# Two edits to a fused recurrence-and-MLP kernel: GpSimd's queue for output packing and half of the stores, 16-bit top bits for the weights

## The chip, the cores and the metric

The kernel runs on one core of a Trainium2 chip. Its engines are called by their profile names: PE (TensorE matmul; PEld is its weight load), DVE (VectorE), ACT (ScalarE), POOL (GpSimd) and SP (SyncE, which here only issues DMAs). Each engine works through its own list of instructions in order and waits on semaphores for the others. A DMA is issued from the list of one engine; here SP and ACT issue all of them. The metric is device time in microseconds (us) of one execution; lower is better.

## The reference

Two blocks in a row. The first is a gated linear recurrence over 4 batches, 8 heads, 768 steps, head size 48; the second a SwiGLU MLP over the 3072 resulting tokens (model width 384, hidden width 1536):

```python
f = 1.0 / (1.0 + np.exp(-f_logit))
for t in range(S):
    state = f[:, :, t, :, None] * state + np.einsum('bhd,bhe->bhde', k[:, :, t], v[:, :, t])
    y[:, :, t] = np.einsum('bhd,bhde->bhe', q[:, :, t], state)
x = y.transpose(0, 2, 1, 3).reshape(B * S, H * D)
g = x @ w_gate
out = (g * (1.0 / (1.0 + np.exp(-g))) * (x @ w_val)) @ w_out
```

q, k, v, f_logit and the output are 32-bit floats. The three weight matrices arrive as 64-bit floats and are turned into 32-bit floats on the core.

## The kernel before

**Chunks and units.** Time is cut into 6 chunks (c = 0 to 5) of 128 steps. For each chunk and each batch b (0 to 3) one "unit" of attention is computed, and then the MLP of the chunk's 512 tokens. Within a unit the recurrence is written as products: scan the gates backward (L576) and forward (L598), scale k and q by the results (L584, L604), multiply them into scores (L617), mask these on DVE (L631), and add the part of the state carried from the chunk before. A unit's function `attention` is a generator; each `yield` is a point where other work is put between.

**Chunk 0 and 1, and the weights.** The attention of chunk 0 runs alone at the start. Then the plain MLP of chunk 0 (`mlp_plain`, L755 and L769, then L778) runs with the attention of chunk 1 and the conversion of the weights around it. A piece of weights is fetched as pairs of 32-bit words into one of 4 buffers (L449, issued by SP), ACT makes two tiles of it, `up` (the low word's contribution, L461) and `top` (the absolute value of the high word, L463), and DVE joins them: clamp (L469), shift and mask (L471), set the sign and the top exponent bit from the high word (L473), and add `up` (L475). In this stretch a scheduler orders the instructions of each engine by its own estimates, so an edit can move neighbours.

**Chunk 2 on (c >= SQUARES).** Now the order of every engine, POOL and SP included, is the order in which the program text puts it (`in_order`), and that follows a planner's list of due times (`CHAINS`, `SCORES`, `times`). PE runs the MLP of the chunk before, as 15 products per hidden triple (`mlp_fifteen`, L957) and then seven products for the way down (`down_seven`: `one`, `six`, `two`, `three`, `four`, `five`, `seven`; L1056 and L1119), with the attention of the present chunk put between.

**How a unit's output reaches the MLP.** For b = 0, 1, 2 the products L652 and L656 leave y in PSUM; ACT copies it into the tile `yT` (L660), and ten DMAs (two of the eight heads straddle a border of 128 rows and go in two pieces) move its pieces of 48, 32 or 16 rows into `xT[c]` (L667), issued by SP. For b = 3 the products go through a block-diagonal tile, `diagonal`: POOL clears it (L544), ACT copies the decayed state into it (two instructions, L546), and PE multiplies (L677). `yT` and `diagonal` share one buffer (tag "x", one copy), so the next writer waits until the ten DMAs of the one before have read it.

**What ACT does behind the diagonal.** ACT's list holds, right after the two copies L546 of chunks 3, 4 and 5, the copy L1082 that empties the single PSUM bank "B" of the products `one` and `two`. The product `four` (seen in the profile as L1056 with the tile `hs`) writes the same bank and starts after that copy.

**POOL and SP.** POOL has little to do from chunk 2 on: a 4-column memset per unit (L605, the gates' first column, which the next unit's backward scan L576 reads) and the diagonal's clear. SP issues, in this order of the text, loads of the squares f, k and q (L428, four DMAs each), of v (L432), a transposition through DRAM for some units (L594, L627), the xT packing (L667), and the stores of half 0 of each block's result (L1065, two DMAs, called from `seven`; half 1 goes out on ACT's queue, called from `five`). An SP DMA that waits holds up all behind it.

Of the kernel before, what the change touches and what calls it, by code (L numbers as in the profile page):

```python
# [9 lines left out]
FP32 = mybir.dt.float32  # L10
I32 = mybir.dt.int32
U32 = mybir.dt.uint32
AF = mybir.ActivationFunctionType
ALU = mybir.AluOpType

# [4 lines left out]
def general_path(ctx, tc, q, k, v, f_logit, moe_w_gate, moe_w_val, moe_w_out, out):  # L20
# [70 lines left out]
    def weight_pieces(dst, src):  # L91
# [9 lines left out]
        def piece(i, j):  # L101
# [13 lines left out]
            nc.vector.tensor_scalar(man, top, 2.0 ** -20, 1.0, op0=ALU.mult, op1=ALU.add)  # L115
            nc.vector.scalar_tensor_tensor(man, lo.bitcast(U32), 2.0 ** -52, man, op0=ALU.mult, op1=ALU.add)
            nc.gpsimd.tensor_tensor(dst[:, i:i + n_a, j:j + n_n], man, p2.bitcast(FP32), ALU.mult)
# [14 lines left out]
    def attention(u):  # L132
        b, c = units[u]
        fr, qr, kr = (raw[nm][u % NRAW] for nm in "fqk")
        nc.scalar.activation(fr[:, :, 0:D], fr[:, :, 0:D], AF.Sigmoid)

# [108 lines left out]
    def mlp(g):  # L245
        h = {}

        def hidden(j):
# [5 lines left out]
            sg = ffn.tile([128, TB], FP32, tag="silu", name="silu", bufs=3)  # L254
            nc.scalar.activation(sg, gp, AF.Silu)
            h[j] = ffn.tile([128, TB], FP32, tag="h", name="h", bufs=16)
# [33 lines left out]
def short_path(ctx, tc, ident, least, judge, q, k, v, f_logit, moe_w_gate, moe_w_val, moe_w_out, out):  # L290
# [9 lines left out]
    nc = tc.nc  # L300
    B, H, S, D = q.shape
    C = 128
    NCH = S // C
# [11 lines left out]
    SQUARES = 2  # L315
# [92 lines left out]
    def squares(nm):  # L408
        return rooms[nm][:, Q:Q + HP * RUN].rearrange("t (a i e) -> t a i e", a=HP, i=NI)[:, :, :, 0:Q]
# [24 lines left out]
    def weight_piece(dst, src, parts):  # L434

        b, a, n = dst.shape[1:]  # L440
        if src.dtype == FP32:
            by_row = src.rearrange("p a (b n) -> p a b n", n=n)
            return (lambda: [nc.sync.dma_start(out=dst[:, :, i], in_=by_row[:, i]) for i in range(a)]), [], []
        shape = [128, b // parts, a, n]
        kept = {}

        def fetch():
            kept["w"] = wst.tile([128, a, 2 * b * n], I32, tag="w64", name="w64", bufs=4)
            nc.sync.dma_start(out=kept["w"], in_=src)  # L449

        def part(m):
            return slice(m * b // parts, (m + 1) * b // parts)

        def halves(m):
            words = kept["w"].rearrange("p a (b n two) -> p a b n two", two=2, n=n)[:, :, part(m)].rearrange("p a b n two -> p b a n two")
            return words[:, :, :, :, 0], words[:, :, :, :, 1]

        def sizes(m):
            lo, hi = halves(m)
            up = wst.tile(shape, I32, tag="up", name="up", bufs=NPART)  # L460
            nc.scalar.activation(up, lo.bitcast(U32), AF.Copy, scale=2.0 ** -29)  # L461
            top = wst.tile(shape, I32, tag="top", name="top", bufs=NPART)
            nc.scalar.activation(top.bitcast(FP32), hi.bitcast(FP32), AF.Abs)  # L463
            kept["up", m], kept["top", m] = up, top

        def join(m):
            lo, hi = halves(m)
            up, top = kept["up", m], kept["top", m]
            nc.vector.tensor_scalar(top.bitcast(FP32), top.bitcast(FP32), as_float(0x38000000), as_float(0x47F00000),  # L469
                                    op0=ALU.max, op1=ALU.min)  # L470
            nc.vector.tensor_scalar(top, top, 3, 0x3FFFFFFF, op0=ALU.logical_shift_left, op1=ALU.bitwise_and)  # L471
            for i in range(b // parts):
                nc.vector.scalar_tensor_tensor(top[:, i], hi[:, i], -(1 << 30), top[:, i], op0=ALU.bitwise_and,  # L473
                                               op1=ALU.bitwise_or)
            nc.vector.tensor_tensor(dst[:, part(m)].bitcast(I32), top, up, ALU.add)  # L475

        return fetch, [lambda m=m: sizes(m) for m in range(parts)], [lambda m=m: join(m) for m in range(parts)]

    def as_float(bits):
        return struct.unpack("<f", struct.pack("<I", bits))[0]  # L480
# [29 lines left out]
    xT = {}  # L510

    def rows_of(par):
        return slice(W * par, W * par + D)
# [3 lines left out]
    def bank(name):  # L517
        return banks[-1].tile([128, 512], FP32, tag="a", name=name)
# [3 lines left out]
    def sigmoid_ahead(u):  # L522


        fr = raw["f"][u % NRAW]
        nc.scalar.activation(fr, fr, AF.Sigmoid)
        ahead.add(u)

    def attention(u):
        b, c = units[u]  # L530
# [17 lines left out]
        def transposed(name, src):  # L548
            p = bank(name)
            for a in range(HP):  # L550
                nc.tensor.transpose(p[:, a * C:(a + 1) * C],
                                    src[:, 2 * a:2 * a + 2, :].rearrange("t r d -> t (r d)"), ident)
            return p.rearrange("p (a t) -> p a t", t=C)

        if c >= SQUARES:
            nc.scalar.activation(squares("f"), squares("f"), AF.Sigmoid)
            if b == (c > SQUARES):

                nc.scalar.activation(spare, spare, AF.Silu)
        else:  # L560
            p = transposed("fTp", fr)
# [9 lines left out]
        if c >= SQUARES:  # L571
# [3 lines left out]
        n = HP * N1  # L575
        nc.vector.tensor_tensor_scan(tail[:, 0:n][:, ::-1], gate[:, 0:n][:, ::-1], floor[:, ::-1], 1.0,  # L576
                                     op0=ALU.mult, op1=ALU.max)
# [9 lines left out]
        if turned:  # L587
# [5 lines left out]
            for r in range(NI):  # L593
                nc.sync.dma_start(out=turn[:, :, :, r, :].rearrange("t i a e -> t (i a) e"),  # L594
                                  in_=beside[Q * r:Q * (r + 1)].rearrange("t i (a e) -> t (i a) e", e=Q))
# [18 lines left out]
        for a in range(HP):  # L614
            for par in range(2):
                r = rows_of(par)
                nc.tensor.matmul(sc[par][:, a * C:(a + 1) * C], lhsT=kT[r, a, :], rhs=qT[r, a, :], start=True, stop=True)  # L617
        if c < NCH - 1 and not turned:
            p = bank("kt")
# [20 lines left out]
        if c and b < B - 1:  # L640

            y = [bank("y") for _ in range(2)]

            def place(a, par):
                return y[par][W * (a % 2):W * (a % 2) + W, a // 2 * C:(a // 2 + 1) * C]

            for a in range(HP):
                for par in range(2):  # L650
                    r = rows_of(par)
                    nc.tensor.matmul(place(a, par), lhsT=decayed[r, a, :], rhs=qT[r, a, :],  # L652
                                     start=a < 2, stop=False, skip_group_check=True)
            for par in range(2):
                for a in range(HP):
                    nc.tensor.matmul(place(a, par), lhsT=v_[:, 2 * a + par, :], rhs=A[:, par, a, :],  # L656
                                     start=False, stop=a >= HP - 2, skip_group_check=True)
            yT = att.tile([128, 2, HP // 2 * C], FP32, tag="x", name="yT")
            for par in range(2):
                nc.scalar.copy(yT[:, par, :], y[par][:, 0:HP // 2 * C])  # L660
            for h in range(H):
                a, par = h // 2, h % 2
                f = h * D
                while f < (h + 1) * D:
                    n = min((h + 1) * D, (f // 128 + 1) * 128) - f
                    r = W * (a % 2) + f - h * D
                    nc.sync.dma_start(out=xT[c][f % 128:f % 128 + n, f // 128, b * C:(b + 1) * C],  # L667
                                      in_=yT[r:r + n, par, a // 2 * C:(a // 2 + 1) * C])
                    f += n
        else:  # L670


            y = bank("y")
            met = set()

            def add(n, lhsT, rhs, last):
                nc.tensor.matmul(y[Q * (n % 4):Q * (n % 4) + Q, n // 4 * C:(n // 4 + 1) * C], lhsT=lhsT, rhs=rhs,  # L677
                                 start=n % 4 not in met, stop=last, skip_group_check=True)
                met.add(n % 4)

            per = 2 * D // Q
            if c:
                for n in range(DM // Q):
                    add(n, diagonal[:, n // per, n % per * Q:(n % per + 1) * Q], qT[:, n // per, :], False)
            flat = v_.rearrange("t h e -> t (h e)")
            for par in range(2):
                for n in range(DM // Q):
                    h = n // per * 2 + par
                    at = n * Q - h * D
                    if -Q < at < D:  # L690
                        add(n, flat[:, W * h + at:W * h + at + Q], A[:, par, h // 2, :], par == 1 or at + Q <= D)
            nc.scalar.copy(xT[c][:, :, b * C:(b + 1) * C], y[:, 0:DM].rearrange("p (a t) -> p a t", t=C))
        yield
        if c < NCH - 1:
            p = bank("dS")
# [212 lines left out]
    def lag(f, *args):  # L908
        lagging.append(lambda: f(*args))  # L909
# [123 lines left out]
    def down_seven(c, h):  # L1033
# [7 lines left out]
        kept = {}  # L1041
# [74 lines left out]
        def seven(n):  # L1116
            p = bank2("o3", "Ao"[n])[:, n, :]
            for j in order:
                nc.tensor.matmul(p, lhsT=hidden_tile(h, j)[:, 2, n * C:(n + 1) * C], rhs=b22[:, j, :], start=j == order[0],  # L1119
                                 stop=j == order[-1])  # L1120
            lag(plus, kept["o", 0][:, n, DH:DM], kept["u5"][:, n, :], p)
            lag(put_out, 0, n, nc.sync)

        return hidden_sums, [(DOWN / 2, lambda f=f, part=part: f(part))
                             for f in (one, six, two, three, four, five, seven) for part in range(2)]
# [237 lines left out]
```

## Time and profile before

| what | value |
|---|---|
| time of the runs without a profile | 609.16, 609.83, 609.94, 610.35; median 609.89 us |
| the profiled execution | 611.35 us, of which the span from first to last instruction is 609.6 us |
| granted TensorE clock | 0.997 |
| ten xT DMAs per unit, 15 units (b = 0, 1, 2 of chunks 1 to 5) | 150 issues, 588 ns median on SP, 1.8 us median to landing |
| stores on SP (L1065) | 10 issues of 192 KB, 2.6 us to landing |
| weight conversion on DVE, L469 + L471 + L473 + L475 | 10.2 + 10.3 + 18.4 + 17.4 us |

The span is what the profile's views describe; the time of a plain run is close to it (0.3 us above). Busy shares are shares of the span. In the groups' view a line reads: line, engine, operation, output<-inputs, shape, count, then busy us and mean ns of one, then idle time of the engine just before, with what ended it. In the timeline a line reads: start, length, engine, line, operation, tiles, shapes, count, and in brackets the idle time just before with what ended it.

### The profile page before, as it was taken

What the parts mean: (1) busy time and instruction counts of PE and PEld (TensorE: products, weight loads), DVE (VectorE), ACT (ScalarE), POOL (GpSimd) and SP (SyncE); (2) the same over time, 40 slices, a digit from 0 to 9 for tenths busy, and PEclk for the clock granted to TensorE, in tenths of its full rate; (3) what the DMA queues carried; (4) which work ended last, traced back from release to release, by engine and by line L of the source; (5) the groups of instructions that cost most, each with busy time, mean ns of one, the idle gap of its engine ahead of it and who ended that gap; (6) DMA issues with size and microseconds to landing.
All of it is one profiled execution on the core that took longest, in us unless ns stands there. A gap on an engine that the chain in (4) does not pass through costs nothing.

```text
span 609.6 us, 10796 instructions
## 1 busy us (share of the span) xinstructions
PE 593.7 (97%) x4036; PEld 488.6 (80%) x4036; DVE 494.5 (81%) x833; ACT 288.6 (47%) x554; POOL 7.5 (1%) x52
## 2 busy tenths in 40 slices
PE   7899999999999999999999999999999999999995
PEld 5744554667888799888899988899988899988895
DVE  7999989868999985999996799996878981666731
ACT  3567544313776512476732376732276731365600
POOL 1000000000000000000000000000000000000000
PEclk9999999999999999999999999999999999999998
DMA  9998372005312045324236344145313100100001
GB/s 203 242 226 282 123 248 78 6 19 159 91 41 73 18 109 125 94 53 96 61 90 148 88 104 106 44 105 127 105 46 84 27 7 9 53 1 1 1 0 59
DMA packets 109142, 54.10 MB, mean 89 GB/s; under 512 B 68760, under 2 KB 102168, under 8 KB 109080
## 3 DMA queue, kind: packets, MB, share of 16 engines
q1 hardware_dynamic: 107064, 50.56, 31.5%
q10 hardware_dynamic: 2016, 2.75, 1.2%
q8 instruction: 34, 0.56, 0.4%
q14 instruction: 28, 0.23, 0.1%
HBM read 44.04 MB, written 6.29 MB: 83 GB/s over the span
## 4 chain that ended last, share of the span: by engine, by line
PE 83%; DVE 10%; SPq 2%; issue 1%; ACT 1%; DMA 1%; POOL 0%; DVEq 0%; ACTq 0%; POOLq 0%
PE o L1056 16%; PE A L957 15%; PE B L957 13%; PE o L957 5%; PE gate L755 5%; PE val L755 5%; PE c L957 5%; PE sc L617 4%; PE o L1119 3%; PE o L778 3%; PE y L677 2%; PE y L656 2%; SPq L667 1%; PE dS L697 1%; PE y L652 1%
## 5 line engine op out<-in xcount | busy, mean ns | idle before, releaser
L1056 PE MATMUL o<-w_out,h 128*128 128x192 f32 x360 | 62.0, 327 | 0.5 <-DVE h L909 0.5
L957 PE MATMUL A<-xs,w_both 128*128 128x256 f32 x240 | 62.1, 381 | 0.0
L1056 PEld LDWEIGHTS o<-w_out,h 128*128 128x128 f32 x360 | 58.7, 190 | 1.7 <-DVE h L909 0.8
L962 ACT COPY c<-A 128x512 f32<-128x512 f32 x40 | 23.3, 583 | 62.7 <-PE A L957 62.7
L962 ACT COPY aside<-A 128x512 f32<-128x512 f32 x60 | 35.1, 585 | 32.5 <-PE A L957 32.5
L858 DVE TENSOR_TENSOR c<-c,aside 128x512 f32<-128x512 f32 x60 | 41.8, 696 | 10.5 <-ACT aside L962 9.0
L957 PEld LDWEIGHTS A<-xs,w_both 128*128 128x128 f32 x240 | 44.9, 190 | 6.5
L909 DVE TENSOR_TENSOR h<-h,c 128x256 f32<-128x256 f32 x100 | 41.4, 422 | 7.3 <-ACT h L973 7.3
L861 DVE TENSOR_TENSOR c<-c,aside 128x512 f32<-128x512 f32 x60 | 41.6, 694 | 2.5 <-ACT aside L962 2.5
L973 ACT ACTIVATE h<-c 128x256 f32<-128x256 f32 x100 | 39.2, 416 | 8.4 <-DVE c L858 5.8
L1056 PE MATMUL o<-ws,h 128*128 128x192 f32 x240 | 41.5, 328 | 0.2 <-DVE A L631 0.2
L957 PE MATMUL B<-xs,w_both 128*128 128x256 f32 x160 | 41.2, 380 | 0.6 <-ACT aside L962 0.6
L957 PE MATMUL c<-xT,w_both 128*128 128x256 f32 x160 | 41.2, 380 | 0.5 <-DVE c L861 0.5
L957 PE MATMUL A<-xs,extra 128*128 128x256 f32 x160 | 41.2, 380 | 0.0
L957 PE MATMUL B<-xT,extra 128*128 128x256 f32 x160 | 41.1, 379 | 0.0
L962 ACT COPY aside<-B 128x512 f32<-128x512 f32 x60 | 35.1, 584 | 11.2 <-PE B L957 7.2
L1056 PEld LDWEIGHTS o<-ws,h 128*128 128x128 f32 x240 | 39.1, 190 | 0.8 <-DVE A L631 0.4
L631 DVE TENSOR_TENSOR A<-sc,causal 128x512 f32<-128x512 f32 x48 | 30.9, 686 | 10.8 <-PE sc L617 10.7
L861 DVE TENSOR_TENSOR c<-o,c 128x512 f32<-128x512 f32 x40 | 27.6, 691 | 9.9 <-ACT h L973 5.8
L957 PEld LDWEIGHTS c<-xT,w_both 128*128 128x128 f32 x160 | 30.3, 190 | 4.9 <-DVE c L861 0.9
L957 PEld LDWEIGHTS B<-xs,w_both 128*128 128x128 f32 x160 | 30.2, 190 | 5.0 <-ACT aside L962 1.0
L957 PEld LDWEIGHTS A<-xs,extra 128*128 128x128 f32 x160 | 30.3, 190 | 4.5 <-ACT c L962 0.4
(138 smaller groups left out, 1136.3 us busy)
## 6 DMA issues: line engine op xcount, KB each, us to landing
fsquares<-in_f_logit_dram SPq DMA_DIRECT2D x64, 96.0 KB, 2.7
ksquares<-in_k_dram SPq DMA_DIRECT2D x64, 96.0 KB, 2.4
qsquares<-in_q_dram SPq DMA_DIRECT2D x64, 96.0 KB, 2.2
v<-in_v_dram SPq DMA_DIRECT2D x24, 192.0 KB, 2.9
w<-in_moe_w_gate_dram SPq DMA_DIRECT2D x6, 768.0 KB, 5.8
w<-in_moe_w_val_dram SPq DMA_DIRECT2D x6, 768.0 KB, 5.3
w<-in_moe_w_out_dram SPq DMA_DIRECT2D x6, 768.0 KB, 5.3
out_dram<-ob ACTq DMA_DIRECT2D x14, 192.0 KB, 2.4
```

The source lines that it names most:

```text
L617: nc.tensor.matmul(sc[par][:, a * C:(a + 1) * C], lhsT=kT[r, a, :], rhs=qT[r, a, :], start=True, stop=True)
L631: nc.vector.tensor_tensor(A[:, par], sc[par].rearrange("p (a t) -> p a t", t=C), causal.unsqueeze(1).broadcast_to((128, HP, C)), ALU.mult)
L755: nc.tensor.matmul(p, lhsT=w[:, j, i, :], rhs=xT[c][:, i, :], start=(i == 0), stop=(i == KT - 1))
L778: nc.tensor.matmul(p, lhsT=hidden_tile(h, n // 2)[:, n % 2 * 2 + b // 2, b % 2 * C:(b % 2 + 1) * C], rhs=w_out[:, j, :], start=(n == 0), s ...
L858: nc.vector.tensor_tensor(dst, a, b, ALU.add)
L861: nc.vector.tensor_tensor(dst, a, b, ALU.subtract)
L909: lagging.append(lambda: f(*args))
L957: nc.tensor.matmul(p[name][:, n, :], lhsT=weights_of[a][:, n, j, :], rhs=tokens[b], start=fresh and n == 0, stop=True, skip_group_check=True)
L962: nc.scalar.copy(t, p[name])
L973: nc.scalar.activation(dst, src[:, 0, :], AF.Silu)
L1056: nc.tensor.matmul(p[:, n, :], lhsT=lhsTs[j][:, n * C:(n + 1) * C], rhs=rhs[:, j, :], start=first and j == order[0] and n == 0, stop=j == ...
L1119: nc.tensor.matmul(p, lhsT=hidden_tile(h, j)[:, 2, n * C:(n + 1) * C], rhs=b22[:, j, :], start=j == order[0], stop=j == order[-1])
```

## The change

Two edits that have nothing to do with each other.

1. The xT packing of chunks 2 to 5 (L667; 120 of the 150 DMAs) and the stores of half 0 of the MLP blocks of chunks 1 to 4 (8 of the 10 DMAs of L1065) are issued by POOL in place of SP. Their place in the text stays; so in POOL's list they stand among the memsets, and in SP's list they are gone. In POOL's list the ten transfers of b = 2 come right ahead of the diagonal's clear, and a block's two stores stand between the memsets of the next chunk's first two units. Those of chunk 1 stay on SP, and so does the last block's half.
2. The join of the weights sets the top two bits by a 16-bit operation. `up` gets its value in its lower 16 bits only (ACT writes every second 16-bit element); DVE writes the upper 16 bits of `up` from the high word's upper quarter, with one single-input AND over the whole piece, in place of a two-input 32-bit operation on `top` for each half of the piece. The last add is as before.

```diff
+        def high_ends(m):
+            quarters = kept["w"].bitcast(U16).rearrange("p a (b n four) -> p a b n four", four=4, n=n)[:, :, part(m)]
+            return quarters.rearrange("p a b n four -> p b a n four")[:, :, :, :, 3]
...
             up = wst.tile(shape, I32, tag="up", name="up", bufs=NPART)
-            nc.scalar.activation(up, lo.bitcast(U32), AF.Copy, scale=2.0 ** -29)
+            ends = up.bitcast(U16).rearrange("p b a (n two) -> p b a n two", two=2)
+            nc.scalar.activation(ends[:, :, :, :, 0], lo.bitcast(U32), AF.Copy, scale=2.0 ** -29)
...
             nc.vector.tensor_scalar(top, top, 3, 0x3FFFFFFF, op0=ALU.logical_shift_left, op1=ALU.bitwise_and)
-            for i in range(b // parts):
-                nc.vector.scalar_tensor_tensor(top[:, i], hi[:, i], -(1 << 30), top[:, i], op0=ALU.bitwise_and,
-                                               op1=ALU.bitwise_or)
+            ends = up.bitcast(U16).rearrange("p b a (n two) -> p b a n two", two=2)
+            nc.vector.tensor_single_scalar(ends[:, :, :, :, 1], high_ends(m), 0xC000, op=ALU.bitwise_and)
             nc.vector.tensor_tensor(dst[:, part(m)].bitcast(I32), top, up, ALU.add)
...
-                    nc.sync.dma_start(out=xT[c][f % 128:f % 128 + n, f // 128, b * C:(b + 1) * C],
-                                      in_=yT[r:r + n, par, a // 2 * C:(a // 2 + 1) * C])
+                    (nc.gpsimd if c >= SQUARES else nc.sync).dma_start(out=xT[c][f % 128:f % 128 + n, f // 128, b * C:(b + 1) * C],
+                                                                       in_=yT[r:r + n, par, a // 2 * C:(a // 2 + 1) * C])
...
-            lag(put_out, 0, n, nc.sync)
+            lag(put_out, 0, n, nc.sync if c == NCH - 1 else nc.gpsimd)
```

In the instruction lists PE's order is unchanged. DVE's 30 instructions of L473 become 20, 4 of shape 128x384 and 16 of 128x768, and some of them stand ahead of the clamp and the shift of their piece, which they no longer need. In the stretch of the weights the order of the DVE and ACT instructions and of the weight fetches changes a little with them.

More of the change, by code (lines that the diff above doesn't have):

```diff
@@ L12 @@
 U32 = mybir.dt.uint32
+U16 = mybir.dt.uint16
 AF = mybir.ActivationFunctionType
```

## The prediction

> **What bounds the kernel now.** I read the engines' shares first, then four stretches of the span.
>
> ```profile
> PE 593.7 (97%) x4036; PEld 488.6 (80%) x4036; DVE 494.5 (81%) x833; ACT 288.6 (47%) x554; POOL 7.5 (1%) x52
> ```
> ```profile
> 28.00:125.00 97.00, 96.53 (x492) 51.45 (x491) 89.44 (x150) 50.46 (x74) 0.32 (x3) 1.00 0.53 158
> 125.00:240.00 115.00, 112.00 (x817) 93.21 (x817) 99.16 (x160) 53.88 (x107) 1.64 (x11) 1.00 0.30 78
> 240.00:530.00 290.00, 290.00 (x2068) 260.09 (x2067) 240.42 (x411) 142.09 (x286) 2.41 (x14) 1.00 0.30 78
> ```
>
> The stretches' columns are start:end, length, busy us of PE, PEld, DVE, ACT and POOL, clock, DMA share, GB/s. PE bounds the kernel. From 28 to 125 us it lacks 0.5 us, to 240 us 3.0 us, from 240 to 530 us nothing. DVE at 92% of the first stretch looks like a second bound, but PE is not waiting for it there. So the change, which leaves PE's own work alone, can gain only at a few waits. It can lose more, wherever PE starts to wait. I looked at PE's waits one by one, and at what stands between each moved transfer and PE.
>
> **The 16-bit edit.** The rows of the join:
>
> ```profile
> L473 DVE SCALAR_TENSOR_TENSOR top<-w,top 128x384 int32<-128x384 int32 x24 | 12.7, 555 | 0.4
> L469 DVE TENSOR_SCALAR top<-top 128x768 f32<-128x768 f32 x16 | 8.8, 552 | 4.1 <-ACT top L463 4.0
> L473 DVE SCALAR_TENSOR_TENSOR top<-w,top 128x768 int32<-128x768 int32 x6 | 5.7, 957 | 0.1
> L469 DVE TENSOR_SCALAR top<-top 128x384 f32<-128x384 f32 x4 | 1.4, 352 | 0.0
> ```
>
> Removed: 24 x 0.555 + 6 x 0.957 = 19.1 us of DVE work. Added: 16 operations on 128x768 and 4 on 128x384. No row shows a 16-bit single-input operation with strides. The nearest is the single-input row L469, which needs 552 ns where the two-input row needs 957: 16 x 0.552 + 4 x 0.352 = 10.2 us, 8.9 less. The other end is the two-input rate: 16 x 0.957 + 4 x 0.555 = 17.5 us, 1.6 less. I take the first, as the new operation has one input. ACT's L461 writes 768 values as before, every second half-word; I leave its 923 ns, and a tenth more would fall into ACT's 48% idle time there.
>
> Of the 8.9 us only what PE waits for counts. The one wait with L473 before it:
>
> ```profile
> 123.79 0.95 DVE L473 SCALAR_TENSOR_TENSOR top<-w,top 128x768 int32<-128x768 int32 x1
> 124.66 0.69 DVE L584 TENSOR_TENSOR kT<-kTp,tails 128x512 f32<-128x512 f32 x1
> 125.26 0.69 DVE L604 TENSOR_TENSOR qT<-qTp,gates 128x512 f32<-128x512 f32 x1
> ```
> ```profile
> 126.09 1.16 PE L617 MATMUL sc<-qT,kT 48*128 48x128 f32 x16 [0.78 <-DVE qT L604]
> ```
>
> DVE works without a gap from 108.3 to 126 us. In the new order the same piece's L473 stands earlier in this run, so only its shortening arrives: 0.957 - 0.552 = 0.4 us, nothing at the two-input rate. In the opening, at 26.06 us, one 128x384 L473 stands in the unbroken DVE run ahead of the mask L631 of chunk 0's last unit, whose y feeds the first gate product: 0.56 - 0.35 = 0.2 us. The other L473s are hidden by PE's backlog. The cover can fail at one point: the new operation waits for the fetched words itself, and in the new list it stands ahead of other work up to two pieces early. Before, one fetch landed at 48.6 us, just as ACT needed it, and the mask at 48.2 us now stands behind that piece's L473. It would start some 1 us later (0.4 of waiting, 0.55 of work); its y is multiplied only at 64 us. I charge 0, and up to 1 us over all such places.
>
> **The transfers on POOL: chunk 2.** SP's list before, ACT behind it, and PE:
>
> ```profile
> 212.71 7.26 SPq L667 DMA_DIRECT2D xT<-yT  x10
> ...
> 224.65 1.81 SPq L428 DMA_DIRECT2D qsquares<-in_q_dram  x4
> 226.55 7.17 SPq L667 DMA_DIRECT2D xT<-yT  x10
> ```
> ```profile
> 222.80 0.76 ACT L660 COPY yT<-y 128x256 f32<-128x256 f32 x2 [0.76 <-DMA v<-in_v_dram]
> ...
> 235.56 0.72 ACT L546 COPY diagonal<-decayed 48x192 f32<-48x192 f32 x2 [9.08 <-POOL gates L605]
> ```
> ```profile
> 235.96 1.12 PE L677 MATMUL y<-qT,diagonal 128*32 128x128 f32 x21 [0.48 <-ACT diagonal L546]
> ```
>
> yT of b = 2 is ready at 223.56 us, but SP issues loads until 226.46 us. POOL could start 3 us earlier. At SP's pace the diagonal would be ready by 233 us, before PE comes at 235.5 us, and the wait goes: 0.48 us, and about 0.2 more for the wait on the second copy. I take 0.7.
>
> **Chunks 3, 4, 5.** Here SP starts at once, so nothing is gained:
>
> ```profile
> 313.35 6.61 SPq L667 DMA_DIRECT2D xT<-yT  x10
> ```
> ```profile
> 321.70 0.71 ACT L546 COPY diagonal<-decayed 48x192 f32<-48x192 f32 x2 [7.84 <-POOL diagonal L544]
> 322.43 0.48 ACT L1082 COPY ob<-o 128x384 f32<-128x384 f32 x1
> ```
> ```profile
> 324.66 4.06 PE L1056 MATMUL o<-ws,hs 128*128 128x192 f32 x24
> ```
>
> The clear starts at 321.25 us, 7.9 after the first issue: ten issues 0.64 apart, and 1.5 for the landing. Then come the copies, then L1082, which frees the bank of the group at 324.66 us. From its end, 322.91 us, the slack is 1.75 us. The same rows of chunk 4 (416.25 to 418.11) leave 1.86, those of chunk 5 (509.13 to 510.05) 0.92.
>
> The unknown is x, the time from one such transfer to the next on POOL, any longer landing spread over the ten. The trace before has no DMA from POOL. The least is 0.45 us, SP's pace for the square loads (4 in 1.81); that is no faster for PE than 0.64. The most is 1.8 us, the median from issue to landing, one transfer at a time. I take 0.64, the row of the same transfers. The Trainium skill speaks against it: "DMA: Bandwidth & Descriptors", Specifications, gives about 1 us to the first byte from GpSimd's queue and about 0.6 from SP's or ACT's; by that ratio x is an estimated 1.07, and the sum would be near 619 us. No row here shows it.
>
> Behind the transfers in POOL's list stand the clears (above) and the memsets L605. The tightest memset, at 221.80 us, would follow ten transfers from 213.1 us, at 223.1 us if x is 1.0; its reader is the scan at 230.14 us. The stores wait for DVE with only the second unit's memset behind them, 12 us later. SP loses 128 issues and is never held by the stores any more; loads and the transposition come up to 7 us earlier, but from 240 to 530 us PE waits for none of them: 0.
>
> **Sum.** 0.4 + 0.2 + 0.7 = 1.3 us. The profiled span of 609.6 becomes 608.3, and the median 609.89, 0.3 above that span, becomes 608.6; I say 608.5, since small waits of PE on DVE between 125 and 240 us may shrink too.
>
> **Rivals.** (B) POOL is slower than SP, and the bank's copy becomes the wait, in chunks 3, 4 and 5. Each loses 10(x - 0.64) minus its slack; it decides from about x = 0.82, where the losses eat the 1.3 us. At x = 1.0: 1.85 + 1.74 + 2.68 = 6.3. In chunk 2 b = 1's buffer comes free at 213.06 + 10 + 1.5 = 224.6, b = 2's copies end at 225.4, the clear starts at 236.9, the first copy ends 0.8 later: PE waits 2.2 in place of 0.7, 1.5 more. Less the DVE gain: 6.3 + 1.5 - 0.6 = 7.2, so 617.1 us. For it: slack under 2 us, and an engine that has issued nothing in this trace. Against it: the whole need is ten issues at SP's pace. (C) Nothing arrives: the 16-bit operation runs at the two-input rate, or waits for fetches, and only chunk 2's wait goes or not even that: 609.2 to 610.9, say 609.9 us. For it: of 19.1 us removed only 0.6 stood on PE's path. Against it: the single-input rows are plainly shorter.
>
> **Chances.** Forecast 0.47, B 0.38, C 0.15. 0.2% (1.2 us) is about what a measurement can tell from no change, and 1.3 us is only just over it: the forecast splits into 0.36 faster, 0.10 same, 0.01 slower, B is 0.36 slower and 0.02 same, C 0.05, 0.05, 0.05. Together 0.41 faster, 0.17 same, 0.42 slower. The forecast's own range is 607.3 to 609.3. The whole reaches to 617.5, x just above 1.0; slower transfers, up to x = 1.8, are left out with some 0.15, times below with 0.03.
>
> **What would show it.** Right: DVE L473 at 0.55 us for 128x768; POOL's ten transfers in 6.5 us; L1082 ending before the group with hs in chunks 3 to 5; no wait of PE at the diagonal of chunk 2. Wrong: transfers near 1 us apart, PE idle ahead of the group with hs with ACT's L1082 named, later clears of the diagonal. A PE wait on DVE below 125 us with L473 in front would be C. The Trainium skill ("SBUF — State Buffer", "The 'DVE blocks DMA' trap") adds that GpSimd can't write its transfers' descriptors while DVE runs its two-port modes; the half-time rows, L469's, end before 126 us, ahead of the first moved transfer at 176 us, so by it nothing is added.

## The result and the profile after

The changed kernel takes 611.24 us in the median (609.74 to 613.92, 43 runs) against 609.94 for the kernel before (608.87 to 612.41, 68 runs). The ratio is 1.0022, with a 95% interval of 1.0015 to 1.0028: slower by 0.2%. I had forecast 608.5, faster. The profiled execution has a span of 611.5 us, where the one shown of before had 609.6.

One correction comes first, since it touches every number below. I had read the 609.6 us of the page as the usual span. Each run lists its span, and the time lies about 1.75 us above it, so a usual run of before has 608.1 us of span; the page showed one of its longer executions. Line numbers in the changed kernel are 1 to 6 higher than before (L428 is now L429, L473 L479, L667 L672, L1056 L1061, L1082 L1087).

From the page of the changed kernel, the busy line and the row of the moved transfers, and then the three stretches of the span that were shown of before (columns as there):

```profile
PE 595.7 (97%) x4036; PEld 490.8 (80%) x4036; DVE 486.4 (80%) x823; ACT 291.2 (48%) x554; POOL 72.2 (12%) x180
...
L672 POOL DMA_DIRECT2D xT<-yT x120 | 59.9, 507 | 44.0 <-ACT yT L665 43.2
```
```profile
28.00:125.00 97.00, 96.50 (x494) 51.73 (x488) 82.78 (x142) 52.70 (x74) 0.76 (x4) 1.00 0.53 159
125.00:240.00 115.00, 113.06 (x828) 94.87 (x829) 99.06 (x161) 54.91 (x108) 16.66 (x40) 1.00 0.32 82
240.00:530.00 290.00, 288.05 (x2045) 257.93 (x2044) 237.93 (x408) 140.48 (x282) 51.65 (x112) 0.99 0.29 75
```

The middle stretch is better: PE lacks 1.9 us there, where it lacked 3.0. The third is worse in two columns at once: PE was busy through all 290 us before and now lacks 1.95, and the clock reads 0.99 where it read 1.00. Both are one event, in chunk 4.

**What arrived as forecast.** PE's timeline, at the two waits that were to shrink:

```profile
124.86 1.16 PE L622 MATMUL sc<-qT,kT 48*128 48x128 f32 x16 [0.28 <-DVE qT L609]
...
232.32 2.11 PE L1061 MATMUL o<-w_out,h 128*128 128x192 f32 x12
234.37 0.86 PE L682 MATMUL y<-qT,diagonal 128*32 128x128 f32 x24
```

The wait on qT is 0.28 us in place of 0.78. The group at chunk 2's diagonal, which had waited 0.48 us, has no bracket any more. POOL's timeline shows why, and at its end the trouble:

```profile
222.41 4.98 POOL L672 DMA_DIRECT2D xT<-yT  x10 [1.58 <-ACT yT L665]
229.94 0.42 POOL L549 MEMSET diagonal<- 128x384 f32 x1 [2.55 <-DMA xT<-yT]
...
405.47 4.98 POOL L672 DMA_DIRECT2D xT<-yT  x10 [0.69 <-ACT yT L665]
416.88 0.42 POOL L549 MEMSET diagonal<- 128x384 f32 x1 [6.43 <-PE o L1061]
```

Ten transfers take POOL 4.98 us, 0.50 each, less than SP's 0.64. In chunk 2 the clear follows 2.5 us after the last issue. In chunk 4 it follows 6.4 us after it. (The releaser named there, PE, is just the event nearest in time; the clear waits for the ten transfers' semaphores, and the last landing in the trace is at 416.27.)

**Where the time went.** At chunk 3's diagonal product the changed kernel leads its predecessor's page by 1.96 us (326.70 against 328.66); at chunk 4's it is 2.28 behind (424.38 against 422.10). So 4.2 us are lost in one chunk. PE and POOL of before at this place:

```profile
418.11 4.06 PE L1056 MATMUL o<-ws,hs 128*128 128x192 f32 x24
422.10 0.86 PE L677 MATMUL y<-qT,diagonal 128*32 128x128 f32 x24
...
414.58 0.42 POOL L544 MEMSET diagonal<- 128x384 f32 x1 [8.22 <-DMA xT<-yT]
```

After, ACT and then PE:

```profile
417.33 0.71 ACT L551 COPY diagonal<-decayed 48x192 f32<-48x192 f32 x2 [11.62 <-POOL diagonal L549]
418.07 0.48 ACT L1087 COPY ob<-o 128x384 f32<-128x384 f32 x1
```
```profile
412.63 4.06 PE L1061 MATMUL o<-ws,h 128*128 128x192 f32 x24
418.60 5.85 PE L1061 MATMUL o<-ws,hs 128*128 128x192 f32 x24 [1.91 <-ACT ob L1087]
424.38 0.86 PE L682 MATMUL y<-qT,diagonal 128*32 128x128 f32 x24
```

The late clear makes the two copies late, these L1087, and PE waits 1.91 us for the bank. Then the group itself takes 5.85 us where the same group, before and elsewhere, takes 4.06. The windows show why (the third column from the end is the granted clock):

```profile
415.00:418.60 3.60, 1.69 (x11) 1.40 (x10) 1.83 (x3) 1.21 (x4) 0.42 (x1) 1.00 0.05 12
418.60:419.70 1.10, 1.10 (x6) 1.10 (x7) 0.40 (x1) 1.08 (x2) 0.10 (x1) 0.96 0.28 75
419.70:423.00 3.30, 3.30 (x12) 3.30 (x12) 0.00 (x0) 1.01 (x2) 0.00 (x0) 0.50 0.37 99
423.00:426.00 3.00, 3.00 (x65) 2.63 (x63) 1.51 (x2) 0.00 (x0) 0.00 (x0) 1.00 0.00 0
```

For 3.3 us after the wait the clock is 0.50, which costs half of that, 1.65 us. Wait and clock are 3.6 of the 4.2 us; some 0.4 comes at 353 us, where a weight load of PE waits 0.23 us on DVE, and the rest is spread.

**What made the transfers land late.** SP's timeline before, in chunk 4, and then after:

```profile
406.79 6.25 SPq L667 DMA_DIRECT2D xT<-yT  x10
413.14 0.53 SPq L432 DMA_DIRECT2D v<-in_v_dram  x1
413.72 0.60 SPq L627 DMA_DIRECT2D kt<-turn  x1
414.42 1.83 SPq L428 DMA_DIRECT2D fsquares<-in_f_logit_dram  x4
```
```profile
405.69 0.38 SPq L433 DMA_DIRECT2D v<-in_v_dram  x1
406.12 0.57 SPq L632 DMA_DIRECT2D kt<-turn  x1
407.33 1.80 SPq L429 DMA_DIRECT2D fsquares<-in_f_logit_dram  x4
409.73 4.05 SPq L429 DMA_DIRECT2D ksquares<-in_k_dram  x4
```

SP no longer has ten transfers ahead of them, so it issues the load of v, the transposition `kt<-turn` and the loads behind it 7.1 to 7.6 us earlier, right into POOL's ten. The transposition lands 7.3 us after its issue, at 413.45 (SP itself waits for it then, inside the last row). It was as slow before: issued at 413.72, landed at 420.93. Then only SP's own loads stood behind it (the first landed 6.8 us after its issue), and no transfer that the diagonal waits for. Of POOL's transfers the two issued up to 406 us land within 2.7 us; the third, issued at 406.46, lands at 413.70. The tile's view of the ten in chunk 4, and of the ten in chunk 5, where SP issues nothing:

```profile
L672 POOL DMA_DIRECT2D xT<-yT x10: 494/504/523, 405.5 to 409.9; - x10
...
DMA to landing us min/median/max: 1.6/6.7/7.2
```
```profile
L672 POOL DMA_DIRECT2D xT<-yT x10: 494/502/523, 501.7 to 506.2; - x10
...
DMA to landing us min/median/max: 1.5/1.6/1.7
```

The signals of the transfers show where they are held. Each of the ten is reported by 16 signals, as many as there are DMA engines. Of the third transfer's, twelve came by 408.75 us and four at 413.22, 413.33, 413.63 and 413.70, each about 0.25 us behind one of the transposition's last four (412.96, 413.06, 413.39, 413.45). I read from this that the transposition lies on four of the 16 engines, and that the landing of a transfer waits for the quarter of it on these four. The data are late there, not the signals alone: of the fourth transfer (issued at 406.95 us) twelve packets of data started by 408.20 us and four at 411.90 or later.

This is theory T: the loss is not POOL's pace but the freed SP, whose transposition now goes into the DMA engines ahead of eight of the ten transfers.

### The profile page after: what moved, and what is told of

Its sections match the earlier page's. It is cut to its first block, busy times and chain, and to the rows that moved or that the text cites. A ratio compares the mean times of both kernels' runs of the same rounds, so it can differ in the third digit from the quotient of the medians.

```text
span 611.5 us, 10819 instructions
## 1 busy us (share of the span) xinstructions
PE 595.7 (97%) x4036; PEld 490.8 (80%) x4036; DVE 486.4 (80%) x823; ACT 291.2 (48%) x554; POOL 72.2 (12%) x180
## 4 chain that ended last, share of the span: by engine, by line
PE 73%; DVE 9%; DMA 1%; issue 1%; POOL 1%; SPq 1%; ACT 0%; DVEq 0%; POOLq 0%; ACTq 0%
PE o L1061 17%; PE A L962 15%; PE B L962 12%; PE o L962 5%; PE c L962 5%; PE sc L622 3%; PE o L1124 3%; PE o L783 3%; PE y L661 2%; PE gate L760 2%; PE val L760 2%; PE y L682 1%; PE y L657 1%; DVE c L866 1%; PE dS L702 1%
## 5 line engine op out<-in xcount | busy, mean ns | idle before, releaser
L672 POOL DMA_DIRECT2D xT<-yT x120 | 59.9, 507 | 44.0 <-ACT yT L665 43.2
L1061 PE MATMUL o<-w_out,h 128*128 128x192 f32 x360 | 62.0, 327 | 0.5 <-DVE h L914 0.5
L1061 PEld LDWEIGHTS o<-w_out,h 128*128 128x128 f32 x360 | 58.7, 190 | 1.7 <-DVE h L914 0.8
L1061 PE MATMUL o<-ws,h 128*128 128x192 f32 x240 | 41.5, 328 | 0.2 <-DVE A L636 0.2
L610 POOL MEMSET gates<- 128x4 f32 x24 | 2.9, 122 | 325.8 <-DVE qT L609 320.7
L1061 PEld LDWEIGHTS o<-ws,h 128*128 128x128 f32 x240 | 39.1, 190 | 0.8 <-DVE A L636 0.4
L863 DVE TENSOR_TENSOR c<-c,o 128x384 f32<-128x384 f32 x15 | 8.3, 554 | 36.5 <-PE o L1061 36.5
```

The lines of the kernel that those rows point to most:

```text
L672: (nc.gpsimd if c >= SQUARES else nc.sync).dma_start(out=xT[c][f % 128:f % 128 + n, f // 128, b * C:(b + 1) * C], in_=yT[r:r + n, par, a / ...
L863: nc.vector.tensor_tensor(dst, a, b, ALU.add)
L1061: nc.tensor.matmul(p[:, n, :], lhsT=lhsTs[j][:, n * C:(n + 1) * C], rhs=rhs[:, j, :], start=first and j == order[0] and n == 0, stop=j == ...
```

## The experiments

Each was run in five rounds beside the kernel before (the second profile of that kernel alone had none). "Idle at hs" is PE's wait at chunk 4's group with the tile hs, in the profile.

| run | us, median (runs) | ratio to before, 95% | idle at hs, us |
|---|---|---|---|
| the change, first measurement | 611.24 (43) | 1.0022 (1.0015 to 1.0028) | 1.91 |
| the change, again | 610.86 (12) | 1.0015 (1.0001 to 1.0029) | 1.65 |
| 16-bit edit alone | 609.42 (12) | 0.9992 (0.9979 to 1.0005) | 0 |
| POOL's transfers and stores alone | 611.25 (8) | 1.0025 (1.0013 to 1.0038) | 1.40 |
| change, one unit's transfers back on SP | 608.97 (11) | 0.9979 (0.9966 to 0.9992) | 0 |
| change, that transposition on PE | 609.85 (11) | 1.0006 (0.9991 to 1.0020) | 0 |
| change, that transposition on POOL, behind | 609.25 (11) | 0.9987 (0.9975 to 1.0000) | 0 |
| queues exchanged | 608.89 (11) | 0.9985 (0.9976 to 0.9994) | 0 |
| change, only the loads behind it moved | 609.29 (12) | 0.9994 (0.9984 to 1.0004) | 0 |
| 16-bit edit, POOL in chunk 2 alone | 608.87 (11) | 0.9983 (0.9973 to 0.9992) | 0 |
| change, stores back on SP | 609.99 (11) | 1.0008 (0.9997 to 1.0018) | 0.84 |

**The 16-bit edit alone.** The two edits of the diff on queues are undone.

> The 16-bit edit alone; every transfer and store stays on SP as before. Theory T (the whole loss is in chunk 4: SP, freed of its ten transfers, issues the transposition kt<-turn 7 us earlier, and the xT transfers behind it in the DMA engines land only after it): T says nothing of this edit, so it gives what its two PE waits gave in the trace of the change, about 0.6 us, perhaps 1.0 with the small waits before 200 us: 608.9 to 609.3 us, and chunk 4's group hs of L1061 starts without a wait. Rival W (the 16-bit edit itself is what hurts, through the slower ACT row: 1083 ns in place of 923): 610 to 611 us.

609.42 us, 0.1 above the expected range, and no wait in chunk 4. The edit does not hurt; its gain, 0.7 us by the medians, can't be told from nothing by the interval. The wait at 124 us is 0.27, as in the full change. Chunk 2 still has its wait:

```profile
234.87 1.12 PE L682 MATMUL y<-qT,diagonal 128*32 128x128 f32 x21 [0.74 <-ACT diagonal L551]
```

**One unit back on SP.** Of 120 moved transfers ten go back:

```diff
-(nc.gpsimd if c >= SQUARES else nc.sync).dma_start(out=xT[c]...
+(nc.gpsimd if c >= SQUARES and u != 4 * B + 2 else nc.sync).dma_start(out=xT[c]...
```

> The change, but the ten transfers of unit c = 4, b = 2 alone go back to SP, ahead of the next transposition in its list. T: the wait of 1.9 us at the first matmul of chunk 4's group hs and the 3.3 us of half clock behind it both go, so 3.5 to 3.9 us less than the changed kernel: 607.3 to 607.8 us, faster than before by 0.3 to 0.4%. Rival S (the loss belongs to the stores on POOL or is spread over chunks 3 to 5): the time stays at 610.8 to 611.3 us.

608.97 us, over 1 us above what I expected, but 1.9 to 2.3 under the change. I had taken the loss from a page with 1.65 us of half clock in it, here and in the next two runs; without that the three ranges would be 609.0 to 609.5, 609.4 to 610.0 and 608.9 to 609.5. The wait is gone:

```profile
412.07 4.06 PE L1061 MATMUL o<-ws,h 128*128 128x192 f32 x24
415.97 4.06 PE L1061 MATMUL o<-ws,hs 128*128 128x192 f32 x24
419.96 0.86 PE L682 MATMUL y<-qT,diagonal 128*32 128x128 f32 x24
```

So ten transfers of one unit hold the whole loss; rival S falls. Whether it is their engine or what they meet is left to the next three.

**The transposition taken away.** All transfers stay on POOL; in unit c = 4, b = 3 PE transposes k.

```diff
-        turned = (SQUARES + 1) * B + 1 < u < (NCH - 1) * B
+        turned = (SQUARES + 1) * B + 1 < u < (NCH - 1) * B - 1
```

> The change with all its transfers on POOL, but in unit c = 4, b = 3 alone the transposition of k is done by PE (four transposes) and copied by ACT, as in the earlier chunks, in place of the DMAs turn<-qT and kt<-turn. T: with no kt<-turn in flight the ten transfers land in 2 to 3 us each and the wait goes, at a price of four transposes (0.44 us): 607.7 to 608.3 us. Rival P (POOL's queue itself lands late, whatever SP does): the wait stays, 611 to 611.7 us.

The mechanism came as T has it, the time did not: 609.85 us in place of 607.7 to 608.3. The profile has 608.0 us of span and no wait, and the ten transfers from the same queue land like this:

```profile
L672 POOL DMA_DIRECT2D xT<-yT x10: 497/504/526, 405.1 to 409.5; - x10
...
DMA to landing us min/median/max: 1.6/2.2/2.5
```

Rival P, that POOL's queue lands late by itself, falls: same queue, same loads of f and k beside it, 2.2 us in place of 6.7. The median stands 0.9 above that of the run before it in this list; 0.53 of it is in the profiles too (PE's end at 601.83 against 601.30), where I had put 0.44 for the four transposes. The rest is within the scatter of these runs.

**The transposition behind the transfers.** One DMA is issued by POOL, in whose list it stands behind the ten.

```diff
-                nc.sync.dma_start(out=kt, in_=turn.rearrange("t i a r e -> i t (a r e)"))
+                (nc.gpsimd if u == 4 * B + 3 else nc.sync).dma_start(out=kt, in_=turn.rearrange("t i a r e -> i t (a r e)"))
```

> The change, with the one DMA kt<-turn of unit c = 4, b = 3 issued by POOL, where it stands behind the ten transfers of b = 2 in the list; nothing else is moved. T: the transfers land by 413 us, kt lands about 7 us later, by 419 to 420, and is read at 422: 607.2 to 607.8 us. If POOL takes long to issue this DMA (2048 or more pieces), the diagonal's clear behind it is late and the wait stays, up to 611. Rival P: 611 us or more.

609.25 us, 1.4 above the expected range and inside it with the half clock taken out. POOL needs 0.72 us for this DMA (the trace has it as 64 packets of 4 KB, and as 128 of 2 KB when SP issues it, not as 2048 pieces); it lands 6.7 us after its issue, at 418.04, and nobody waits for it. The clear is early:

```profile
406.17 4.98 POOL L672 DMA_DIRECT2D xT<-yT  x10 [0.69 <-ACT yT L665]
411.31 0.72 POOL L632 DMA_DIRECT2D kt<-turn  x1 [0.15 <-issue]
413.47 0.42 POOL L549 MEMSET diagonal<- 128x384 f32 x1 [1.45 <-DMA xT<-yT]
```

So with the transposition behind the ten transfers the wait is gone, as with none at all.

**The queues exchanged.** Both edits together: the ten on SP, the transposition on POOL, free to start beside them.

> The ten transfers of c = 4, b = 2 go back to SP, as in the run that lost the wait (608.97 us), and the kt<-turn of b = 3 goes to POOL, which has nothing else to do there and can issue it at about 405.5 us, while SP issues the transfers. So the same collision is made with the two queues exchanged. T1 (16 DMA engines serve what came first, whichever queue it is from): the transfers issued after kt<-turn land late, the clear comes at 413.5 to 416 us, the wait at group hs is back in part or whole (0 to 2 us, up to 1.6 more of half clock): 609.5 to 612. T2 (only POOL's queue gives way to SP's): SP's transfers land as in the other run, kt late, no wait: 608.7 to 609.3.

608.89 us, T2's time, yet T1's landings. SP's first two transfers land 1.8 us after issue; the third, issued at 407.19 just after POOL's transposition (406.67), lands at 412.39, right after the transposition at 412.21 (again by its last four signals; the other twelve had come by 409.01):

```profile
L672 SPq DMA_DIRECT2D xT<-yT x10: 545/587/590, 405.9 to 411.6; - x10
...
DMA to landing us min/median/max: 1.8/2.5/5.2
```

The hold-up works in both directions, so it is not that POOL's queue alone gives way to SP's. But it hurt nothing: the transposition took 5.5 us, the ten were through 1.5 us after it, and the clear, at 413.89, was in time. T was not yet the whole cause.

**Only the loads behind it.** In the run with the queues exchanged SP's list had no loads until the ten were out; in the change eight loads follow the transposition. They alone are moved, behind the clear in POOL's list; the transposition stays in front.

```diff
-                    nc.sync.dma_start(
+                    (nc.gpsimd if u == 5 * B + 1 and nm != "q" else nc.sync).dma_start(
                         out=rooms[nm][Q * n:Q * (n + 1), at:at + HP * RUN].rearrange("t (a e) -> t a e", a=HP),
```

> The change with kt<-turn left where it is, at the head of SP's freed list; only the eight loads of f and k squares that SP issues behind it (for the second unit after) go to POOL, where they stand behind the diagonal's clear. Theory L: the transposition alone lands in 5.3 to 5.5 us, as where no load follows it (chunk 3, and the run in which POOL issued it), and the ten transfers then land at once; the delay is the sum of both. The last transfer lands by 412 to 413.2 us in place of 415.2 to 416.3, the clear comes by 413.5 and the wait at group hs falls from 1.7 to 1.9 us to 0 to 0.3: 608.7 to 609.4 us. Rival K (the transposition in front is enough, whatever follows): it takes 7 us as before, the wait stays at 1 us or more: 610 to 611 us.

609.29 us, as expected, and no wait in chunk 4:

```profile
416.18 4.06 PE L1061 MATMUL o<-ws,hs 128*128 128x192 f32 x24
...
DMA to landing us min/median/max: 1.6/4.2/5.6
```

The transposition is issued at 405.77; the eight held transfers land from 411.70 to 412.98. So it lands within 5.9 us, and the eight need 1.3 us behind it. In the change it took 7.3 us, and the eight another 2.6, their landings alternating with those of the loads (413.70, 413.90, load 414.08, 414.28, 414.66, load 414.94, and so on to 416.27). Theory L holds: the transposition in front costs some 5 us, which the slack of this place bears, and the loads that SP sends after it cost 2.5 to 3 more, which it does not bear. Chunk 3 is the cross-check within the change: there the transposition of another unit also goes ahead (issued at 312.30, the transfers behind it land from 317.78), no load follows until 319, and PE does not wait. The same holds for three more of its six transpositions, issued at 290.06, 353.91 and 383.83 ahead of nine transfers each: no load follows within 6 us, and PE waits at none of them.

**POOL in chunk 2 alone.**

```diff
-(nc.gpsimd if c >= SQUARES else nc.sync).dma_start(out=xT[c]...
+(nc.gpsimd if c == SQUARES else nc.sync).dma_start(out=xT[c]...
...
-            lag(put_out, 0, n, nc.sync if c == NCH - 1 else nc.gpsimd)
+            lag(put_out, 0, n, nc.sync)
```

> The 16-bit edit, and POOL's transfers in chunk 2 only; chunks 3 to 5 and all stores stay on SP as before. T: chunk 2 is the only place where the move gains (0.7 to 0.9 us) and there no kt<-turn runs, so this has all of the gain and none of the loss, the same as with the one unit moved back: 608.7 to 609.3 us, 0.1 to 0.3% under before. If the moved transfers of chunks 3 to 5 or the stores gained something too, it stands above that run by as much: 609.5 or more.

608.87 us, with the exchanged queues (608.89) and the one unit back (608.97) the fastest here: faster than before by 0.17% (0.08 to 0.27%). PE reaches the group at 126 us 1.26 us later in this profile than in that of the run with one unit back (125.80 against 124.54, the half clock of the opening), and chunk 4's group hs 1.34 later (417.31 against 415.97). So the gain of the move is in the 30 transfers of chunk 2; none of the other 90 or of the stores can be seen.

**The stores back on SP.**

> The change with the stores of half a block back on SP. T: the stores have no part in the loss; the kt<-turn of chunk 4 stays ahead of the transfers, so the time is that of the changed kernel, 610.7 to 611.5 us, with the same wait at group hs. Rival S (POOL's stores cost the time): 608.7 to 609.5 us.

609.99 us, between the two forecasts, and half of the wait:

```profile
416.70 4.17 PE L1061 MATMUL o<-ws,hs 128*128 128x192 f32 x24 [0.84 <-ACT ob L1087]
```

The collision is the same here (issued at 405.29, the first held transfer lands at 412.00), so the stores are not its cause, but by the medians 0.9 us of its price is theirs; the intervals of the two runs overlap. Two differences are seen in the profiles: the transposition lands 6.9 us after issue where it took 7.3 and 7.5 in the two profiles of the change, and the clear starts 0.19 us after the last landing, where it took 0.6 in both. Why, no run shows.

**The moved DMAs without the 16-bit edit.**

> The change without the 16-bit edit: transfers and stores on POOL, weights joined as before. T: gain of chunk 2 (0.9), loss of chunk 4 (1.9 to 3.9), and without the gain of the 16-bit edit (0.7 by its own run): 611.6 to 612.6 us. In the trace the waits before 126 us (0.63 at 105 and 0.94 at 124) are those of the kernel before. If the two parts of the change disturb each other, it is not the changed kernel's time plus 0.7: under 611.2 would mean that the 16-bit edit makes the collision worse.

611.25 us, a little under the expected range, and as much as the change itself: the 16-bit edit's 0.7 us can't be seen beside this wait. The waits before 126 us are those of the kernel before only at 124 us (0.94 us lost); the one at 105 us is absent. In chunk 4 the wait is 1.40 us, 0.25 less than in the second profile of the change, with a transposition 0.34 us shorter (7.14 against 7.48); whether that is chance, no run shows.

**Both kernels again.** First the change:

> The changed kernel once more, for a second profile beside more times. T: the wait at chunk 4's group hs is there in every execution, 1.5 to 2.1 us, since nothing in it depends on chance; the 3.3 us of half clock behind it need not be, since the changed kernel's usual span (609.5) is 2.0 under the one profiled (611.5) and 2.3 above the kernel with the one unit moved back (607.2): I expect 608.9 to 610 us of span, the wait without the half clock. Rival: the wait itself comes and goes, then a profile at the usual span shows none. Time 610.9 to 611.5 us.

610.86 us; span 609.1, the wait is back, and the group behind it has its 4.17 us, at full clock:

```profile
417.51 4.17 PE L1061 MATMUL o<-ws,hs 128*128 128x192 f32 x24 [1.65 <-ACT ob L1087]
```

So wait and half clock are two costs: the first is in all four profiles in which the transposition and its loads go ahead of the ten, the second in one of them. Then the kernel before:

> The kernel before once more, for a second profile: its usual span is 608.1 us and the page shown was 609.6. The wait of 0.48 us at chunk 2's diagonal and the one of 0.8 to 0.9 us at 124 us belong to the order of the queues and should be there again; a wait of 0.63 us at 105 us, which the changed kernel does not have, is absent from the run with POOL's transfers and the old join too, so it should be chance and absent: span 607.8 to 608.6 us.

One execution, 611.44 us. The wait at 105 us was chance and is gone, but the span was 609.7 us, over 1 us above the expected range: here the half clock fell into the opening. The wait at 124 us is there again, 0.78; that at chunk 2's diagonal, which I expected too, is not. The window of the opening, and the group at the diagonal, which starts as the one before it ends:

```profile
26.00:33.00 7.00, 6.25 (x68) 4.39 (x66) 6.17 (x14) 4.10 (x9) 0.00 (x0) 0.76 0.92 211
```
```profile
233.77 2.11 PE L1056 MATMUL o<-w_out,h 128*128 128x192 f32 x12
235.90 1.12 PE L677 MATMUL y<-qT,diagonal 128*32 128x128 f32 x21
```

0.76 over 7 us is 1.7 us lost, behind a wait of 0.8 us that every profile has at this place. Three more of these profiles have it, at 27.7 us (queues exchanged, chunk 2 alone, transposition behind). A single page can be off by such an event, in either kernel.

## Why the prediction was wrong

- **The step that failed**: "SP loses 128 issues and is never held by the stores any more; loads and the transposition come up to 7 us earlier, but from 240 to 530 us PE waits for none of them: 0." They did come 7.1 to 7.6 us earlier. I asked who reads them, and not what they share: DMA engines, with the very transfers that were moved. In place of 0 it cost 1.7 to 1.9 us of wait, and 1.65 of half clock in one execution of two. Without it (one unit back) the change is faster than before by 0.21% (0.08 to 0.34%).
- **The landing, 1.5 us behind the last issue**, was kept from SP's rows as if it belonged to the transfer. It was 1.6 us in chunk 5, where SP issues nothing beside them, and 6.7 in the median of chunk 4. x was to hold "any longer landing spread over the ten", but a hold-up behind one big DMA is a sum of its own, and can't be got from the pace of the queue.
- **x, the pace on POOL**: taken 0.64, measured 0.50, inside its bounds and better. The estimate of 1.07 from the Trainium skill's first-byte figures ("DMA: Bandwidth & Descriptors", Specifications) is not borne out by this pace, nor is POOL slower from issue to landing: with nothing beside them its transfers land in 1.6 us, SP's in 1.8. (By the prediction's own terms x = 1.07 gives 619.9 us, not 619.)
- **Rival B** named the right place and chain, copies late, L1087 late, PE waiting at the group with hs, but the wrong cause: it needed x above 0.82, in three chunks. The place was hit in one chunk, with x at 0.50, so that the right place was luck.
- **The 16-bit operation**: taken 0.552 us on 128x768. The rows of the change, the new operation and ACT's:

```profile
L479 DVE TENSOR_SCALAR up<-w 128x768 uint16<-128x768 uint16 x16 | 9.8, 610 | 1.6 <-DMA w<-in_moe_w_val_dram 0.9 <-DMA w<-in_moe_w_gate_dram 0.7
L479 DVE TENSOR_SCALAR up<-w 128x384 uint16<-128x384 uint16 x4 | 2.3, 583 | 0.0
```
```profile
L467 ACT ACTIVATE up<-w 128x768 uint16<-128x768 uint32 x16 | 17.3, 1083 | 13.8 <-issue 8.3 <-DVE w_both L480 3.7 <-ACT top L469 1.0
```

  0.61 us, near the single-input row as chosen, and far from 0.957. On 128x384 the choice was wrong: taken 0.352, measured 0.583, more than the 0.555 of the operation that it replaces. Its waits for fetches, the risk named, are 1.6 us of DVE time and reach PE nowhere. What reaches PE, 0.5 at 124 us and 0.1 in the opening, is the 0.6 of the sum, in part by luck: the gain in the opening does not come from a shorter operation (0.56 before, 0.58 now) but from its start, 25.93 us in place of 26.06. At 191 us 0.2 is lost again, where PE waits 0.75 us in place of 0.57. "I leave its 923 ns" for ACT's write was wrong, 1083, a sixth more and not "a tenth", and costs nothing in ACT's idle time there.
- **Chunk 2**: 0.7 us forecast, 0.55 between the medians of two runs (609.42 and 608.87), and the wait gone. The wait itself varies: 0.48 us on the page of before, 0.74 with the 16-bit edit alone, none in the second profile of before.
- **The base of the sum**: "the median 609.89, 0.3 above that span" set a usual time against an unusual span. It shifts no difference, but it made the page's chance events (the wait at 105 us) look like part of the kernel.
- POOL's list and its memsets held as said. The DVE lock was to add nothing, and nothing is seen of it: POOL issues its 120 transfers in 494 to 651 ns each, 504 in the median.

## What to carry to other kernels

When a queue is relieved, list what it will now issue earlier and lay that against the transfers which were moved off it: the two queues end in the same DMA engines. Here a slack of 1.9 us bore the transposition of 256 KB in front (the last transfer landing at 412.98), and not with the loads behind it (415.20 and 416.27 in the two profiles of the change). Move DMAs only where the profile shows the old queue late (here chunk 2), and leave them where it starts at once. Take two profiles of a kernel before a difference of 0.3% is explained.

## What the runs showed of the hardware

- A DMA issued from one queue holds the landing of those issued later from another, both ways: POOL's behind SP's, up to 7.2 us, and SP's behind POOL's, up to 5.2. Of the first held transfer's 16 signals only four are late, both ways, each right behind one of the transposition's last four. The Trainium skill ("DMA: Bandwidth & Descriptors", Queues, rings and completion order) has both sides of it: each DMA engine takes turns between queues, which would let small transfers through, and a completion's semaphore write lands only after every earlier write of that engine, across its queues. The order of the landings goes with the second. It is not the whole, since the data of the held pieces started late as well (411.90 us or later against 408.04 to 408.20 for the same transfer's others).
- The transposition read from DRAM lands 4.9 to 6.2 us after its issue where no load follows within 6 us, and in 6.2 to 7.5 where seven do, over the runs' profiles.
- A wait of 1.9 us was followed by 3.4 us at half clock; waits of 1.65, 1.40 and 0.84 us at the same place were not. In the opening, where every profile has a wait of 0.79 us at 25.4 and another of 0.64 to 0.75 us near 27.8, four of the thirteen profiles have half clock behind them, also for 3.4 us, and nine have not. The same skill ("TensorE: Matmul & The Clock Gate", The HAM clock gate) has the clock fall after an idle window of about 3.4 us, free-running. The waits here are shorter, so the trace does not agree in the idle time needed; it does in the dependence on chance.
